# Row-tiled transposes, one copying engine, and one weight load on another queue, at the head of a SwiGLU kernel

## The chip, the cores and the metric

The kernel runs on one core of one Trainium2 chip. The time is device microseconds of one execution; the profile is one profiled execution of the same program.

## The reference

```python
# x: [1, 2048, 512], w_gate and w_up: [512, 1376], w_down: [1376, 512], all bf16
def reference(x, w_gate, w_up, w_down):
    g = _silu(x @ w_gate)
    u = x @ w_up
    return (g * u) @ w_down
```

## The kernel before

The 2048 tokens are worked in four chunks of 512. For each chunk the first stage computes the hidden tensor transposed: the 1376 hidden features are cut in ten F tiles of 128 and a rest of 96. For an F tile, TensorE multiplies four weight tiles of 128x128 (over the 512 input features) with the transposed input `xT_sb`, once for gate (a group "G") and once for up (a group "U"). Each group has one of the eight PSUM banks, in turn. ScalarE takes the silu of a gate bank, VectorE multiplies it with the up bank and stores bf16 in `hT_sb`. The rest of 96 features is packed in groups "X" and "Y". The second stage (lines 446 to 477) multiplies `hT_sb` with `w_down`, mostly in row tiles of 32, and stores the output.

Everything is scheduled by hand: each engine has one list of instructions in a fixed order, with waits on counting semaphores. The loads go out in the order written in `loads_on_scalar` and `loads_on_sync`, one hardware queue for each of the two engines. Gate and up weights are cut by F tiles in slabs, `slabs = [(0, 1), (1, 2), (2, 4), (4, 7), (7, NFT)]`: `load_gate(sp, 0, 1)` is the gate weights of F tile 0, and so on.

The head of the kernel concerns chunk 0. TensorE must have its input transposed. For most of x a transposing DMA does that (`load_x`). For the first 256 tokens this would land late, so they are loaded as they are (`load_xn`, two blocks of 128 tokens, `xn0` on SyncE's queue and `xn1` on ScalarE's) and transposed on TensorE against an identity matrix (line 357) into PSUM, and copied from there to `xT_sb`. A block `i` has two halves `h`: half 0 holds input features 0 to 255 (two weight tiles), half 1 the others. One copy moves one half; the copies of half 0 are on VectorE (line 300), those of half 1 on ScalarE (line 288), and `s_X` tells them how many transposes are done. While the loads are in flight TensorE runs matmuls on constants (`warm`, line 346): five of 512 columns and then `N_FILL` = 5 of 128 columns.

TensorE then runs groups 0 to 7 (gate and up of F tiles 0 to 3) for the first 256 tokens, in the order 0, 1, 2, 3, 4, 6, 5, 7: gate 0, up 0, gate 1, up 1, gate 2, gate 3, up 2, up 3. Gate 0 is done in two pieces of 128 tokens, each matmul waiting for the copy that it needs (`xt_ready`, line 336). After that the second 256 tokens of the same groups follow, gate 0 again in two pieces of 128 tokens, the first waiting for the load `x0b`, the second for `x0c`. From group 8 on the groups take all 512 tokens at once.

Of the kernel before, what the change touches and what calls it, by code (L numbers as in the profile page):

```python
# [7 lines left out]
FP32 = mybir.dt.float32  # L8

N_WARM = 5  # L10
N_FILL = 5


def bass_standalone__swiglu_ffn__prompt_kernel(nc, x, w_gate, w_up, w_down, out):
    _, S, D = x.shape
    F = w_gate.shape[1]
    P = 128
    KD = D // P
# [10 lines left out]
    NXN = HT // P  # L29
# [20 lines left out]
    with ExitStack() as es:  # L50
# [4 lines left out]
        xT_sb = sb("xT_sb", [P, KD, S], BF16)  # L55
# [14 lines left out]
        xn_sb = sb("xn_sb", [P, NXN, D], BF16)  # L70
# [3 lines left out]
        s_X = sem("s_X")  # L74
# [8 lines left out]
        def load_sem(name):  # L83
            loads[name] = sem(f"s_{name}")
            return loads[name]
# [6 lines left out]
        def load_x(eng, name, t0, t1):  # L92
            eng.dma_start_transpose(
                xT_sb[:, :, t0:t1], xf[t0:t1, :]
            ).then_inc(load_sem(name), 16)

        def load_w(eng, name, src, base, f0, f1):
            eng.dma_start(
                w_sb[:, :, base + f0:base + f1],
                src[:, f0:f1].rearrange("(k p) f -> p k f", p=P),  # L100
            ).then_inc(load_sem(name), 16)

        slabs = [(0, 1), (1, 2), (2, 4), (4, 7), (7, NFT)]
        slab_of = {ft: a for a, b in slabs for ft in range(a, b)}

        def load_gate(eng, a, b):
            load_w(eng, f"wg{a}", w_gate, 0, a * P, min(b * P, F))

        def load_up(eng, a, b):
            load_w(eng, f"wu{a}", w_up, UPH, a * P, min(b * P, F - 32))  # L110

        def load_xn(eng, i):
            eng.dma_start(xn_sb[:, i, :], xf[i * P:(i + 1) * P, :]).then_inc(load_sem(f"xn{i}"), 16)

        def loads_on_scalar(act):
            load_xn(act, 1)
            load_up(act, *slabs[0])

        def loads_on_sync(sp):
            load_xn(sp, 0)  # L120
            load_gate(sp, *slabs[0])
            for a, b in slabs[1:3]:
                load_gate(sp, a, b)
                load_up(sp, a, b)
            load_x(sp, "x0b", HT, HT + P)
            load_x(sp, "x0c", HT + P, SC)
            for a, b in slabs[3:]:
                load_gate(sp, a, b)
                load_up(sp, a, b)
            load_w(sp, "wut", w_up, F - (F - 32), F - 32, F)  # L130
            for c in range(1, NSC):
                load_x(sp, f"x{c}", c * SC, (c + 1) * SC)
            sp.dma_start(
                wd_sb[:, 0:NFF, :], w_down[0:NFF * P, :].rearrange("(k p) d -> p k d", p=P)
            ).then_inc(load_sem("wd"), 16)
            load_sem("wdt")
            for y0 in (0, 64):
                sp.dma_start(wd_sb[y0:y0 + 64, T01, :], w_down[NFF * P:F - SR, :]).then_inc(loads["wdt"], 16)
            for x0 in range(0, P, SR):
                sp.dma_start(wd_sb[x0:x0 + SR, T2, :], w_down[F - SR:F, :]).then_inc(loads["wdt"], 16)  # L140
            sp.dma_start(wd_sb[0:F_LAST, TAIL, :], w_down[NFF * P:F, :]).then_inc(load_sem("wdl"), 16)
# [12 lines left out]
        def add_op(eng, g, **what):  # L154
            n_read[eng] += 1
            op = dict(g=g, at=n_read[eng], **what)
            (act_ops if eng == "A" else dve_ops).append(op)
            g["readers"].append((eng, op["at"]))
            return op

        RT = [1] * NXN
        T_BANK = [2 * i for i in range(NXN)]

        def tview(i, h):
            n, b0 = RT[i], T_BANK[i] + RT[i] * h
            return bank_all[:, b0:b0 + n, 0:P // n].bitcast(BF16).rearrange("p b (k t) -> p k b t", k=2)

        sg_reader = []
# [42 lines left out]
                t_ready[c] = max(t_ready[c], d["at"])  # L211

        xt_ready = {}
        for i in range(NXN):
            for h, eng in enumerate("DA"):
                op = add_op(
                    eng, dict(readers=[]), kind="copy", ready=(s_X, 2 * sum(RT[:i]) + RT[i] * (h + 1)),
                    out=xT_sb[:, 2 * h:2 * h + 2, i * P:(i + 1) * P].rearrange("p k (b t) -> p k b t", b=RT[i]),
                    src=tview(i, h), stored=(None, 0),
                )  # L220
                xt_ready[i, h] = (eng, op["at"])

        for c in range(NSC):
            for ft in range(NFF):
# [8 lines left out]
        for at, t in enumerate(tiles):  # L233
# [3 lines left out]
            for c0, c1 in parts:  # L237
                g = add_group("O", t=t, c0=c0, c1=c1)
                eng = "A" if at % 2 == 1 and c0 == 0 else "D"
                op = add_op(  # L240
                    eng, g, kind="copy", out=o_sb[ob][:, c0:c1], src=g["bank"][:, 0:c1 - c0],
                    stored=(s_out[ob], need),
                )
# [15 lines left out]
        def on_sync(sp):  # L259
            loads_on_sync(sp)  # L260
            store_tiles(sp, "S")
            for i in range(NOS):
                sp.wait_ge(s_out[i], 16 * n_store[i])
# [11 lines left out]
        def on_scalar(act):  # L275
            loads_on_scalar(act)
            act.activation(adummy[:, 0:4], zero_c, ACT.Silu)
            for op in act_ops:
                act.wait_ge(*ready(op))
                if op["kind"] == "silu":  # L280
                    if op["free"]:
                        act.wait_ge(s_D, op["free"])
                    fn = ACT.Silu
                else:
                    if op["stored"][1]:
                        act.wait_ge(*op["stored"])
                    fn = ACT.Copy
                act.activation(op["out"], op["src"], fn).then_inc(s_A, 1)  # L288
            store_tiles(act, "A")
# [13 lines left out]
        def on_tensor(pe):  # L303
            landed = set()

            def need(name, count=1):
                if name not in landed:
                    pe.wait_ge(loads[name], 16 * count)
                    landed.add(name)
# [34 lines left out]
            def warm(n, width):  # L344
                for i in range(n):
                    pe.matmul(banks[NB - 1][:, 0:width], lhsT=ones_w, rhs=ones_m[:, 0:width], start=True, stop=True)  # L346

            warm(N_WARM, SC)
            warm(N_FILL, P)
            pe.wait_ge(s_I, 1)  # L350
            for i in range(NXN):
                need(f"xn{i}")
                for dk in range(KD):
                    for b in range(RT[i]):
                        rt = P // RT[i]
                        r0 = rt * b
                        ins = pe.matmul(  # L357
                            tview(i, dk // 2)[:, dk % 2, b, :], lhsT=xn_sb[r0:r0 + rt, i, dk * P:(dk + 1) * P],
                            rhs=ident[r0:r0 + rt, r0:r0 + rt], start=True, stop=True, is_transpose=True,
                            tile_position=(r0, 0), skip_group_check=True,  # L360
                        )
                        if dk % 2 == 1:
                            ins.then_inc(s_X, 1)

            first = groups[0:NB]
# [9 lines left out]
            for g in groups[NB:NO]:  # L375
                free(g)
                kind = g["kind"]
# [83 lines left out]
            for g in groups[NO + TPC * (TPC - 1):]:  # L461
                t, c0, c1 = g["t"], g["c0"], g["c1"]
# [5 lines left out]
                for fk in (tailed if last else full[1:]):  # L468
                    if fk < NFF:
                        h, w = hT_sb[:, fk, t * P:(t + 1) * P], wd_sb[:, fk, c0:c1]  # L470
                    else:
                        h, w = hl_sb[0:F_LAST, :], wd_sb[0:F_LAST, TAIL, c0:c1]
# [7 lines left out]
        on_gpsimd(nc.gpsimd)  # L480
        on_scalar(nc.scalar)
        on_tensor(nc.tensor)
        on_vector(nc.vector)

# [27 lines left out]
```

## Time and profile before

| | |
|---|---|
| median of 3 runs | 120.48 us |
| the runs | 120.21, 120.48, 120.73 us |
| the profiled execution | 119.86 us, span 118.6 us |
| PE busy | 115.4 us, 97% of the span |
| VectorE, ScalarE busy | 37.8 us, 34.9 us |
| transposes (line 357) | 8, started from 3.46 us on |
| first matmul of gate 0 (line 337) | 4.36 us |

In the views of the profile, PE is TensorE's matmuls and PEld its weight loads, DVE is VectorE, ACT ScalarE, POOL GpSimd; SPq and ACTq are the issuing sequencers of SyncE and ScalarE. Times are microseconds from the span's start. The name of a weight load in the trace, `w_sb<-in_w_gate_dram` or `w_sb<-in_w_up_dram`, does not say which slab it is; the order of issue does. q1 is the DMA queue of SyncE, q10 that of ScalarE. A matmul's time in the profile includes its way through the array, so neighbouring ones overlap: the distance of their starts is the pace.

### The profile page before, as it was taken

Reading aid. Unit: us, or ns where it says so; the run is one execution under the profiler, and the core shown is the slowest. Engines: PE = TensorE matmul, PEld = TensorE weight load, DVE = VectorE, ACT = ScalarE, POOL = GpSimd, SP = SyncE. Lnnn points to the kernel's source line nnn. Section 1 sums busy time; section 2 is a strip of 40 time slices with the busy share of each in tenths; the row PEclk is TensorE's granted clock in tenths of the full one; section 3 lists DMA queues with packets and bytes.
Section 4 is the critical chain, followed back from the end, with each engine's and each line's share of the span. In section 5 each row is a group of like instructions: output and inputs, shape, how many; then the busy total and the mean of one; then the engine's idle time right before and its main releaser. Section 6 shows DMA issues by size and latency. Waiting matters only on the chain.

```text
span 118.6 us, 2318 instructions
## 1 busy us (share of the span) xinstructions
PE 115.4 (97%) x1004; PEld 60.0 (51%) x1012; DVE 37.8 (32%) x58; ACT 34.9 (29%) x60; POOL 1.1 (1%) x7
## 2 busy tenths in 40 slices
PE   7999999999999999999999999999999999999993
PEld 2888444444444444444444444444444445885442
DVE  0106543344433444424444344360000044003321
ACT  4307324353244272343263432330000033003021
POOL 1000000000000000000000000010000000000000
DMA  3999999994000000000000000000000017200532
GB/s 104 270 200 330 267 172 188 233 358 105 0 6 0 0 0 0 0 0 6 0 0 6 0 0 0 0 0 6 0 6 0 0 57 239 68 0 0 168 103 88
DMA packets 17642, 8.83 MB, mean 74 GB/s; under 512 B 10624, under 2 KB 17632, under 8 KB 17632
## 3 DMA queue, kind: packets, MB, share of 16 engines
q1 hardware_dynamic: 16816, 8.33, 28.1%
q10 hardware_dynamic: 816, 0.36, 1.1%
q8 instruction: 8, 0.13, 0.4%
q14 instruction: 2, 0.02, 0.0%
HBM read 4.75 MB, written 2.10 MB: 58 GB/s over the span
## 4 chain that ended last, share of the span: by engine, by line
PE 97%; issue 1%; DVE 0%
PE bank L337 58%; PE bank L434 25%; PE bank L473 7%; PE bank L385 3%; PE bank L346 2%; PE bank L396 2%; PE bank L357 1%; DVE o_sb L300 0%
## 5 line engine op out<-in xcount | busy, mean ns | idle before, releaser
L337 PE MATMUL bank<-xT_sb,w_sb 128*128 128x512 bf16 (+2 forms) x355 | 69.9, 355 | 0.3
L337 PEld LDWEIGHTS bank<-xT_sb,w_sb 128*128 128x128 bf16 x360 | 34.4, 98 | 34.9
L296 DVE TENSOR_TENSOR hT_sb<-sg_sb,bank 128x512 bf16<-128x512 f32 x40 | 27.5, 688 | 40.5 <-PE bank L337 34.5
L288 ACT ACTIVATE sg_sb<-bank 128x512 f32<-128x512 f32 x40 | 23.8, 596 | 40.9 <-PE bank L337 40.9
L434 PE MATMUL bank<-wd_sb,hT_sb 32*128 32x512 bf16 x496 | 29.0, 374 | 0.0
L434 PEld LDWEIGHTS bank<-wd_sb,hT_sb 32*128 32x128 bf16 x496 | 15.3, 93 | 11.5 <-issue 0.4
L300 DVE CAST o_sb<-bank 128x512 bf16<-128x512 f32 (+1 forms) x10 | 5.7, 595 | 31.1 <-PE bank L434 25.9
L288 ACT ACTIVATE o_sb<-bank 128x512 bf16<-128x512 f32 (+1 forms) x8 | 4.3, 582 | 33.6 <-PE bank L434 27.9
L473 PE MATMUL bank<-wd_sb,hT_sb 128*128 128x512 bf16 (+2 forms) x55 | 7.9, 303 | 0.2 <-issue 0.2
L473 PEld LDWEIGHTS bank<-wd_sb,hT_sb 128*128 128x128 bf16 x56 | 4.2, 98 | 4.2 <-issue 0.4
L434 PE MATMUL bank<-wd_sb,hy_sb 32*128 32x512 bf16 (+1 forms) x32 | 5.0, 371 | 0.0
L385 PE MATMUL bank<-xT_sb,w_sb 128*128 128x512 bf16 x14 | 3.8, 379 | 0.1
L296 DVE TENSOR_TENSOR hx_sb<-sgx_sb,bank 32x512 bf16<-32x512 f32 x4 | 2.8, 691 | 3.5 <-ACT sgx_sb L288 3.5
L288 ACT ACTIVATE sgx_sb<-bank 32x512 f32<-32x512 f32 x4 | 2.4, 588 | 4.5 <-PE bank L385 4.5
L346 PE MATMUL bank<-const-bfloat16-1.0 128*128 128x512 bf16 (+1 forms) x10 | 2.8, 466 | 0.8 <-PEq L497 0.8
L434 PE MATMUL bank<-wd_sb,hx_sb 32*128 32x512 bf16 (+1 forms) x16 | 3.0, 371 | 0.0
L385 PEld LDWEIGHTS bank<-xT_sb,w_sb 128*128 128x128 bf16 x16 | 1.6, 98 | 1.9
L288 ACT ACTIVATE sgy_sb<-bank 64x512 f32<-64x512 f32 x4 | 2.4, 590 | 0.1
L346 PEld LDWEIGHTS bank<-const-bfloat16-1.0 128*128 128x128 bf16 x10 | 1.2, 139 | 2.2 <-issue 2.2
L396 PE MATMUL bank<-xT_sb,w_sb 128*64 128x512 bf16 x16 | 1.9, 382 | 0.0
L434 PEld LDWEIGHTS bank<-wd_sb,hy_sb 32*128 32x128 bf16 x32 | 1.6, 93 | 0.6
L300 DVE COPY xT_sb<-bank 128x256 bf16<-128x256 bf16 x2 | 0.6, 292 | 4.1 <-PE bank L357 3.9
(17 smaller groups left out, 8.9 us busy)
## 6 DMA issues: line engine op xcount, KB each, us to landing
out_dram<-o_sb SPq DMA_DIRECT2D x15, 128.0 KB, 1.8
wd_sb<-in_w_down_dram SPq DMA_DIRECT2D x1, 1280.0 KB, 8.1
w_sb<-in_w_gate_dram SPq DMA_DIRECT2D x1, 480.0 KB, 6.0
w_sb<-in_w_up_dram SPq DMA_DIRECT2D x1, 448.0 KB, 6.7
w_sb<-in_w_gate_dram SPq DMA_DIRECT2D x1, 384.0 KB, 3.9
w_sb<-in_w_up_dram SPq DMA_DIRECT2D x1, 384.0 KB, 4.3
w_sb<-in_w_gate_dram SPq DMA_DIRECT2D x2, 128.0 KB, 3.2
w_sb<-in_w_gate_dram SPq DMA_DIRECT2D x1, 256.0 KB, 3.5
```

The costliest lines, as they stand in the source:

```text
L288: act.activation(op["out"], op["src"], fn).then_inc(s_A, 1)
L296: ins = dve.tensor_tensor(op["out"], op["a"], op["b"], ALU.mult)
L300: ins = dve.tensor_copy(op["out"], op["src"])
L337: ins = pe.matmul(g["bank"][:, n0:n1], lhsT=w_sb[:, dk, col:col + P], rhs=xT_sb[:, dk, c * SC + n0:c * SC + n1], start=(dk == 0), stop=(dk ...
L346: pe.matmul(banks[NB - 1][:, 0:width], lhsT=ones_w, rhs=ones_m[:, 0:width], start=True, stop=True)
L357: ins = pe.matmul(tview(i, dk // 2)[:, dk % 2, b, :], lhsT=xn_sb[r0:r0 + rt, i, dk * P:(dk + 1) * P], rhs=ident[r0:r0 + rt, r0:r0 + rt], s ...
L385: ins = pe.matmul(g["bank"][:, :], lhsT=w_sb[:, dk, XC0:XC0 + P], rhs=xT_sb[:, dk, c * SC:(c + 1) * SC], start=(dk == 0), stop=(dk == KD - 1),
L396: ins = pe.matmul(g["bank"][y0:y1, :], lhsT=w_sb[:, dk, YC0:YC0 + 64], rhs=xT_sb[:, dk, c * SC:(c + 1) * SC], start=(dk == 0), stop=(dk == ...
L434: ins = pe.matmul(g["bank"][:, 0:c1 - c0], lhsT=h, rhs=wd_sb[r0:r0 + SR, w, c0:c1], start=(start and fk == fks[0]), stop=(stop and fk == f ...
L473: ins = pe.matmul(g["bank"][:, 0:c1 - c0], lhsT=h, rhs=w, start=(last and fk == 0), stop=(fk == (NFF if last else NFF - 1)), skip_group_ch ...
```

## The change

Three things. The fills are four instead of five. The load of up of F tile 1 is taken out of SyncE's list, where it stood behind gate 1, and becomes ScalarE's third load, behind `xn1` and up of F tile 0. And the transposes of three of the four halves are done in two row tiles of 64 tokens each: a half is then four transposes of 64 columns instead of two of 128, the two row tiles writing to two PSUM banks; the last half (block 1, half 1) keeps its two of 128. All four copies are on VectorE.

```diff
-N_FILL = 5
+N_FILL = 4
...
         def loads_on_scalar(act):
             load_xn(act, 1)
-            load_up(act, *slabs[0])
+            for a, b in slabs[:2]:
+                load_up(act, a, b)
 
         def loads_on_sync(sp):
             load_xn(sp, 0)
             load_gate(sp, *slabs[0])
-            for a, b in slabs[1:3]:
-                load_gate(sp, a, b)
-                load_up(sp, a, b)
+            load_gate(sp, *slabs[1])
+            load_gate(sp, *slabs[2])
+            load_up(sp, *slabs[2])
             load_x(sp, "x0b", HT, HT + P)
             load_x(sp, "x0c", HT + P, SC)
...
-        RT = [1] * NXN
-        T_BANK = [2 * i for i in range(NXN)]
+        halves = [(i, h) for i in range(NXN) for h in range(2)]
+        RT = {ih: 1 if ih == halves[-1] else 2 for ih in halves}
+        t_bank, t_count, nb, nt = {}, {}, 0, 0
+        for ih in halves:
+            t_bank[ih] = nb
+            nb += RT[ih]
+            nt += RT[ih]
+            t_count[ih] = nt
 
         def tview(i, h):
-            n, b0 = RT[i], T_BANK[i] + RT[i] * h
+            n, b0 = RT[i, h], t_bank[i, h]
...
         xt_ready = {}
-        for i in range(NXN):
-            for h, eng in enumerate("DA"):
-                op = add_op(
-                    eng, dict(readers=[]), kind="copy", ready=(s_X, 2 * sum(RT[:i]) + RT[i] * (h + 1)),
-                    out=xT_sb[:, 2 * h:2 * h + 2, i * P:(i + 1) * P].rearrange("p k (b t) -> p k b t", b=RT[i]),
-                    src=tview(i, h), stored=(None, 0),
-                )
-                xt_ready[i, h] = (eng, op["at"])
+        for i, h in halves:
+            op = add_op(
+                "D", dict(readers=[]), kind="copy", ready=(s_X, t_count[i, h]),
+                out=xT_sb[:, 2 * h:2 * h + 2, i * P:(i + 1) * P].rearrange("p k (b t) -> p k b t", b=RT[i, h]),
+                src=tview(i, h), stored=(None, 0),
+            )
+            xt_ready[i, h] = ("D", op["at"])
...
-            for i in range(NXN):
+            for i, h in halves:
                 need(f"xn{i}")
-                for dk in range(KD):
-                    for b in range(RT[i]):
-                        rt = P // RT[i]
+                rt = P // RT[i, h]
+                for k in range(2):
+                    dk = 2 * h + k
+                    for b in range(RT[i, h]):
                         r0 = rt * b
                         ins = pe.matmul(
-                            tview(i, dk // 2)[:, dk % 2, b, :], lhsT=xn_sb[r0:r0 + rt, i, dk * P:(dk + 1) * P],
+                            tview(i, h)[:, k, b, :], lhsT=xn_sb[r0:r0 + rt, i, dk * P:(dk + 1) * P],
                             rhs=ident[r0:r0 + rt, r0:r0 + rt], start=True, stop=True, is_transpose=True,
                             tile_position=(r0, 0), skip_group_check=True,
                         )
-                        if dk % 2 == 1:
+                        if k == 1:
                             ins.then_inc(s_X, 1)
```

## The prediction

> **What bounds the kernel now.** The page comes first: PE is busy for 115.4 of the 118.6 us, and the chain that ended last is PE for 97%. So a change pays only where PE waits. The chain of waits in order of time begins so (start us, us, what, count):
>
> ```profile
> 0.84 2.82 PE bank L346 x10
> 3.67 0.76 PE bank L357 x8
> 4.43 7.44 PE bank L337 x72
> 11.87 0.05 issue
> 11.92 10.31 PE bank L337 x47
> ```
>
> The change touches the first two pieces and the loads that feed the third. From 11.92 us PE needs 0.216 us for a matmul of 512 columns (10.36 us for the 48 of a neighbouring piece) and goes on so. Next the timeline of the head (start us, us, engine line):
>
> ```profile
> 2.27 0.51 SPq L98 DMA_DIRECT2D w_sb<-in_w_up_dram  x1
> ...
> 3.46 0.97 PE L357 MATMUL bank<-ident,xn_sb 128*128 128x128 bf16 x8
> 3.92 0.72 DVE L300 COPY xT_sb<-bank 128x256 bf16<-128x256 bf16 x2 [3.92 <-PE bank L357]
> ...
> 4.13 0.72 ACT L288 ACTIVATE xT_sb<-bank 128x256 bf16<-128x256 bf16 x2 [0.89 <-PE bank L357]
> ```
>
> Eight transposes start at 3.46; four copies follow on two engines, the last ending at 4.85 (4.13 + 0.72). The same timeline has gate 0's first matmul at 4.36 and up 0's first at 5.03. Gate 0's eight 128-column matmuls thus take 0.67 us. Undisturbed ones start 0.056 apart (four from 8.11 to 8.27 in a narrow window), 0.45 for eight, so gate 0 loses 0.22 us waiting for pieces of xT.
>
> Third, the loads, each in a window of its own, as issue time plus time to landing: xn 0 at 3.2, xn 1 at 3.4, gate 0 at 1.26 + 3.0 = 4.3, up 0 at 4.8, gate 1 at 1.73 + 3.4 = 5.1, up 1 at 2.27 + 3.3 = 5.6, slab 2 to 4 of gate at 2.83 + 3.5 = 6.3 and of up at 7.1, x0b at 3.92 + 3.9 = 7.8, x0c at 5.32 + 3.1 = 8.4. Gate 0's matmuls start 0.06 after gate 0 lands. From 5.03 to 8.11 PE runs 28 matmuls of 256 columns, 0.11 each, 0.44 for a group of four: gate 1 at 5.47, up 1 at 5.91, gate 2 at 6.35, gate 3, up 2, up 3, then gate 0's second half at 8.11. Set beside the landings: gate 2 begins 0.05 after its slab lands, and the last quarter of gate 0 (ideal start 8.33) begins at 8.42, 0.05 after x0c. PE is following the loads. The stretches, with DMA share and GB/s last, say why:
>
> ```profile
> 4.50:5.00 0.50, 0.50 (x8) 0.32 (x7) 0.14 (x1) 0.35 (x2) 0.00 (x0) 1.00 1.24 289
> ...
> 7.00:7.50 0.50, 0.50 (x7) 0.44 (x6) 0.00 (x0) 0.00 (x0) 0.00 (x0) 1.00 1.21 251
> 7.50:8.00 0.50, 0.50 (x8) 0.44 (x6) 0.00 (x0) 0.00 (x0) 0.00 (x0) 1.00 0.30 51
> ```
>
> From 2.5 to 7.5 us the 16 DMA engines are full (share 1.05 to 1.29 in every half microsecond), and they run dry only when x0c's packets are through. These loads are bound by bandwidth, not by issue. After 8.42 nothing stops PE again: slab 4 lands at 10.5 and is wanted at 11.7.
>
> **The change, part by part.** The profiled execution took 119.86 us: its span of 118.6 and 1.26 around it. The median of the runs shown is 120.48, 0.62 above; I work out shifts in the span and add them to the median.
>
> *One fill less.* Five fills run 2.93 to 3.67, starts 0.107 apart ((0.74 - 0.31) / 4). xn 0 is there at 3.2, so transposes may start at 3.36: 0.107 gained.
>
> *Transposes in row tiles.* Eight of 128 columns at 0.107 (0.86 us) become twelve of 64 columns and two of 128. By column count a short one is 0.053 (0.427 for 512, 0.107 for 128). Whether two of them run together no row shows for 64 rows. The nearest shows it for 32: 540 matmuls of line 434 in 29.41 us, 0.054 each where 512 columns alone take 0.216. So six pairs cost 0.32, plus 0.21 for the last two: 0.53, or 0.33 gained. Unpaired, 0.85: nothing. If a short one costs as much as a long one, 14 x 0.107 = 1.50: 0.64 lost. I take pairs.
>
> Against it stands the change of tile shape, twice (128 to 64 rows, and back for the last two). The timeline shows two such changes at full pace (last column of the first row: 16 matmuls):
>
> ```profile
> 77.42 1.92 PE L396 MATMUL bank<-xT_sb,w_sb 128*64 128x512 bf16 x16
> 79.27 0.40 PE L434 MATMUL bank<-wd_sb,hT_sb 32*128 32x512 bf16 x4
> ```
>
> Eight pairs at 0.216 are 1.73; from 77.42 to 79.27 are 1.85, so a change of shape costs about 0.10. PE here still runs at half pace (0.107 against 0.056), so 0.10 to 0.20 each; I take 0.10, by the row. The first eats the fill's 0.107: row tiles start at 3.46 as the transposes do now.
>
> *Copies, all on VectorE.* Each is 0.292 on VectorE (0.384 on ScalarE). Queued one behind another they overlap by 0.09 (two hy_sb multiplies of 0.683 fit in 1.29), so four take 0.92, or 1.17 without overlap. Reading two banks may be slower: the f32 casts give 0.224 for 64 columns and 0.688 for 512, 1.04 ns a column, so 0.42 for 256 without packing, and 1.4 to 1.7 for four. I take 0.292. The first half's last pair starts at 3.51, ends 0.26 later (0.311 less 0.053); the copy starts at 3.81; the last ends between 4.73 and 4.98, against 4.85 now. Two engines gave the same with eight slower transposes: the shorter transposes pay for the lost engine, and little is left. Gate 0 can't start before its weights, 4.3, anyway. Up 0 starts at 4.90 to 5.15; I take 4.95, 0.08 earlier. Behind the copies VectorE has nothing until the multiply at 9.56.
>
> *Up 1 on ScalarE.* The issue (0.5) goes ahead of the table load (1.74 to 3.02, then to about 3.5) and the dummy activation (to 3.7). ScalarE's next work is the silu at 8.85, now that its copies are gone: 5 us of cover, cost nothing. Every later SyncE issue comes 0.55 earlier. But the engines are full, and the bytes ahead of x0c are the same, so x0c lands where it did, give or take 0.1.
>
> What moves is the order. Up 1 used to follow gate 1 alone on SyncE's queue. Now it shares the engines, behind up 0, whose packets end about 4.3 (ScalarE's queue moves almost nothing from 4.25 on). While both queues worked, they shared nearly evenly:
>
> ```profile
> q1 hardware_dynamic: 518, 0.13, 59.3%
> q10 hardware_dynamic: 399, 0.11, 49.1%
> ```
>
> (2.75 to 3.75 us.) At 4.25 some 0.03 MB of gate 1 are left; they then take 0.25 us (0.06 MB at 250 GB/s) beside as much of up 1. The other 0.1 MB of up 1 go beside slab 2 to 4 of gate: 0.6 us at an even share, 0.9 at a third (its packets are 256 bytes beside 512). Packets end at 5.1 to 5.4, and a landing comes 0.65 after the last packet, as now (4.9 to 5.6): 5.8 to 6.1, 0.2 to 0.5 later than today. PE wants it at 4.95 + 0.88 = 5.83. I take 5.85 and a start at 5.90, against 5.91 now. Gate 2's slab, with the same bytes ahead of it, lands at 6.3 as before: PE at 6.35 as before, the last quarter at 8.42 as before.
>
> **Sum:** 0.08 gained at gate 0 is lost again at up 1 or gate 2; whatever is left is lost at x0c. Net 0.0, bounds -0.15 to +0.2: 120.5 us.
>
> **The rivals.** *Faster: x0c and the slabs land with their issue.* If the landing follows the issue, x0c comes up to 0.55 earlier and the 0.09 before the last quarter goes, with gate 0's 0.13 kept: 120.26. For it: x0c lands 1.8 us after its issue ends (5.32 + 1.26 = 6.58), as quickly as an output store. Against it: full engines until 7.5.
>
> *Slower: up 1 lands late.* The change says beside gate 1; it may land half a microsecond after it. At 6.1, up 1 starts at 6.15 and gate 2 at 6.59, 0.24 late, of which x0c's 0.09 hides a part: +0.15, 120.6. If slab 2 of up or x0c also slips by 0.2: 120.8. It decides once up 1 lands after 5.86. The Trainium skill (DMA: Bandwidth & Descriptors, Queues, rings and completion order) says that an engine alternates between queues by packets of several descriptors, not by bytes; by that up 1 gets the third and this rival holds. The window above (0.13 against 0.11 MB) had equal packet sizes on both queues for most of it and can't tell.
>
> *Slower: row tiles that don't overlap.* At 0.107 for each and slow copies, up 0 starts near 6.0: +0.97, less 0.09: 121.4. It decides once up 0 starts after 5.12. Against it: the rows of lines 434 and 396.
>
> *Slower: the clock.* Transpose starts are 0.107 apart, gate 0's 0.056: PE doubles its pace near 4.2, about 3.3 us after its first matmul, though the clock column reads 1.00 throughout. Now PE idles a little between the last transpose (4.1) and gate 0. If the half pace lasted another 3.3 us, half of that is lost: +1.65, 122.1. Against it: 0.2 us of idling in 3.3 is little. The Trainium skill (TensorE: Matmul & The Clock Gate, Part 4) says that a transpose does not count as PE activity in the way of a matmul; by that the stretch that counts shrinks from 2.62 us (0.84 to 3.46) to 2.51, which speaks for this rival. In the trace of before the pace doubled right after eight transposes, so those at least did not prevent it.
>
> **How the numbers follow.** No net change 0.64; faster by landings 0.14; up 1 late 0.10; row tiles alone 0.05; clock 0.07. The three runs spread 0.52 us. The likeliest is 120.5. The range, 119.95 (the faster case with half that spread) to 121.0 (late up 1 with it), leaves out the clock and about half of the row tiles and some 0.04 of tails. About 0.5%, 0.6 us, is what a measurement of this kernel can tell from no change: slower than that are the clock and most of the row tiles, 0.11; faster, past the 0.31 us that gate 0 (0.22) and x0c (0.09) lose now, only with the spread, 0.05; the rest, 0.84, within.
>
> **What would show it.** Right: row tiles from about 3.46 in pairs 0.05 apart, the last copy ending 4.7 to 5.0, up 0 at 4.9 to 5.1, up 1 landing at 5.8 or later, gate 2 near 6.35, the last quarter of gate 0 near 8.4. Wrong: x0c landing before 8.0, up 1 before 5.6, gate 2's slab before 6.1, or a pace of 0.107 beyond 4.4.

## The result, and the profile after

The changed kernel takes 120.85 us (median of 21 runs), the kernel before 120.48 us (also 21). The ratio is 1.003, with a 95% interval of 1.0016 to 1.0043: about 0.36 us slower. That is within the 0.5% that was forecast as most likely, on its slow side, and the interval tells it from no change at all. (One run of the changed kernel, 122.55 us, was a slow one and is not in the ratio.)

The profiled execution after has a span of 119.2 us against 118.6. Its chain of waits in order of time (start us, us, what, count) begins:

```profile
0.84 2.72 PE bank L352 x9
3.56 0.13 issue
3.69 0.83 PE bank L364 x14
4.53 18.34 PE bank L343 x120
```

Line 352 is the fills, 364 the transposes, 343 the gate and up groups (346, 357 and 337 before). There is no wait for a load in it. The transposes start at 3.69 us, not at 3.46, behind 0.13 us of waiting. From there on the chain shows no break in PE; it hides short ones, since neighbouring matmuls overlap, as the 0.18 us for which the first weight load of gate 0 waits. The timeline of the head:

```profile
1.25 1.08 ACTq L98 DMA_DIRECT2D w_sb<-in_w_up_dram  x2
1.26 1.52 SPq L98 DMA_DIRECT2D w_sb<-in_w_gate_dram  x3
2.36 1.28 ACT L283 ACT_TABLE_LOAD   x1 [2.36 <-issue]
...
3.69 0.83 PE L364 MATMUL bank<-ident,xn_sb 64*128 64x64 bf16 x14
4.03 0.89 DVE L306 COPY xT_sb<-bank 128x256 bf16<-128x256 bf16 x4 [4.03 <-PE bank L364]
4.44 4.62 PEld L343 LDWEIGHTS bank<-xT_sb,w_sb 128*128 128x128 bf16 x40 [0.18 <-DMA w_sb<-in_w_gate_dram]
```

Twelve short transposes start 0.026 apart (3.69 to 3.96), so two share a slot; four copies fit in 0.89 us. But gate 0 and what follows run at half pace: in the stretch from 5.3 to 6.2 us, and in the one from 6.7 to 8.7, the groups of PE are (count | busy us, mean ns):

```profile
L343 PE MATMUL bank<-xT_sb,w_sb 128*128 128x256 bf16 x5 | 1.2, 408 | 0.0
```

```profile
L343 PE MATMUL bank<-xT_sb,w_sb 128*128 128x256 bf16 x21 | 2.5, 273 | 0.0
```

The mean time of a matmul does not give the pace, the distance of the starts does: until about 6.2 us matmuls of 256 columns start 0.21 us apart, then 0.11. In the profile of before full pace was there from gate 0's first matmuls, at 4.36 us. Taken alone, these two profiles would say that the clock made the kernel slower. The experiments show that one kernel has the long half pace in one execution and not in the next, that the loss is there without it, and that it can be there without the loss.

Two executions are too few for this head. In thirteen profiles of kernels that differ only there, the span is always 106.9 us plus the start of group 8 (11.71 before, 12.35 after). All differences arise before that.

### The profile page after: what moved, and what is told of

Its sections match the earlier page's. It is cut to its first block, busy times and chain, and to the rows that moved or that the text cites. A ratio compares the mean times of both kernels' runs of the same rounds, so it can differ in the third digit from the quotient of the medians.

```text
span 119.2 us, 2336 instructions
## 1 busy us (share of the span) xinstructions
PE 116.5 (98%) x1017; PEld 60.2 (50%) x1017; DVE 38.2 (32%) x60; ACT 34.2 (29%) x58; POOL 1.1 (1%) x7
## 4 chain that ended last, share of the span: by engine, by line
PE 98%; DVE 0%; issue 0%
PE bank L343 59%; PE bank L441 25%; PE bank L480 7%; PE bank L392 3%; PE bank L352 2%; PE bank L403 2%; PE bank L364 1%; DVE o_sb L306 0%
## 5 line engine op out<-in xcount | busy, mean ns | idle before, releaser
L343 PE MATMUL bank<-xT_sb,w_sb 128*128 128x512 bf16 (+2 forms) x360 | 70.7, 359 | 0.0
L343 PEld LDWEIGHTS bank<-xT_sb,w_sb 128*128 128x128 bf16 x360 | 35.1, 99 | 34.8 <-DMA w_sb<-in_w_gate_dram 0.2
L392 PEld LDWEIGHTS bank<-xT_sb,w_sb 128*128 128x128 bf16 x16 | 1.6, 98 | 1.9
```

The source lines that it names most:

```text
L343: ins = pe.matmul(g["bank"][:, n0:n1], lhsT=w_sb[:, dk, col:col + P], rhs=xT_sb[:, dk, c * SC + n0:c * SC + n1], start=(dk == 0), stop=(dk ...
L392: ins = pe.matmul(g["bank"][:, :], lhsT=w_sb[:, dk, XC0:XC0 + P], rhs=xT_sb[:, dk, c * SC:(c + 1) * SC], start=(dk == 0), stop=(dk == KD - 1),
```

## The experiments

The theories after the two profiles: *clock* (idle time before gate 0 brings the half pace back), *loads* (up 1 and what is behind it land later), *chance* (the two executions differ by accident).

**The changed kernel again.**

> The changed kernel once more, for a second profile. Clock theory: PE's pace falls back to half (0.107 us for 128 columns, 0.21 for 256) somewhere between 4.4 and 6.5 us again, and the span is 119.2 to 119.9 us, 120.85 us in the timing. Load theory (the late x0c and up 1 set the time): the pace is full from about 4.2 us on, and PE waits at up 1 and at the last quarter of gate 0. Chance theory (the profiled execution had slow loads at 2.0 to 2.5 us by accident): xn 0 lands at 3.2 and the head looks like that of before.

120.75 us, ratio to before 1.0025 (1.0011 to 1.004). PE is at full pace at 4.5 us here, and still the span is 119.5 us. The clock theory's half pace did not come back; xn 0 landed at 3.57, so this was not a head like the first one of before either. Its chain of waits:

```profile
1.71 0.03 issue
1.74 5.10 DMA w_sb<-in_w_up_dram
6.84 0.05 issue
6.88 5.86 PE bank L343 x56
```

The chain goes back through ScalarE's third load: up 1 is issued at 1.74 and lands at 6.84. The same profile's timeline shows both stops, at gate 1 and at up 1:

```profile
6.03 0.61 PE L343 MATMUL bank<-xT_sb,w_sb 128*128 128x256 bf16 x4 [0.33 <-DMA w_sb<-in_w_gate_dram]
...
6.88 2.36 PE L343 MATMUL bank<-xT_sb,w_sb 128*128 128x256 bf16 x20 [0.24 <-DMA w_sb<-in_w_up_dram]
```

**Transposes of 128 tokens.**

```diff
-        RT = {ih: 1 if ih == halves[-1] else 2 for ih in halves}
+        RT = {ih: 1 for ih in halves}
```

> The changed kernel with all transposes of 128 tokens (eight, as before); one fill less, copies on VectorE and up 1 on ScalarE stay. Clock theory: the transposes take 0.86 us instead of 0.5 and fill the gap before gate 0, so the half pace does not come back; 0.2 to 0.5 us faster than the changed kernel, about 120.5. Load theory: no difference from the changed kernel, 120.8.

120.67 us, ratio 1.0018 (1.0003 to 1.0033), not to be told from the changed kernel. PE was at full pace from about 4.5 us, and stood waiting for gate 1 (6.23) and up 1 (6.93). The eight transposes cost 0.107 each again, and it made no difference.

**Up 1 back on SyncE's queue.**

```diff
-            for a, b in slabs[:2]:
-                load_up(act, a, b)
+            load_up(act, *slabs[0])
...
-            load_gate(sp, *slabs[1])
-            load_gate(sp, *slabs[2])
-            load_up(sp, *slabs[2])
+            for a, b in slabs[1:3]:
+                load_gate(sp, a, b)
+                load_up(sp, a, b)
```

> The changed kernel with up of F tile 1 back in SyncE's list behind gate 1. Load theory: up 1 lands 0.3 to 0.5 us earlier (5.6 to 5.8) and the kernel gains 0.2 to 0.4 us, to 120.5. Clock theory: the half pace after 4.4 us stays, 120.8 within 0.15 us.

120.41 us, ratio 1.000 (0.9983 to 1.0018): the loss is gone. Up 1 landed at 5.66, 0.62 after gate 1. The half pace lasted until 6.2 us in this profile, as in the first one after. In this execution it cost about 0.5 us: slab 2 to 4 of gate landed at 6.50, and PE came to it at 7.08. The median of the 12 runs is none the slower for it.

**Five fills.**

> The changed kernel with five fills of 128 columns instead of four. Clock theory: the gap before the transposes closes by 0.107 us and part of the gain of a busy PE comes back: 0.1 to 0.4 us faster than the changed kernel, 120.5. Load theory: no difference, 120.8; the fill ends at 3.46, before xn 0 can be used where it lands late.

120.65 us, ratio 1.0023 (1.0006 to 1.004): the same as with four. In this profile the row tiles started at 3.69 again, behind xn 0 at 3.56; the number of fills does not set their start.

**The kernel before again, and the move alone.**

> The kernel before, for a second profile. If the first profile's early input (xn 0 at 3.22 us) was an accident, xn 0 lands near 3.57 us here as in the four others, and the span is near 119.2 us, gate 1 at 5.0 to 5.2 and up 1 at 5.5 to 5.7 as before. If early input belongs to that kernel, 3.2 again and a span of 118.6.

Span 119.3 us, xn 0 at 3.68. The first profile of before was an early execution. Here gate 1 landed at 5.91 and not at 5.1 (a miss of both expectations), up 1 at 6.36, and the chain of waits goes through slab 2 to 4 of gate ("slab 2" from here on):

```profile
2.27 0.51 SPq L98
2.78 0.04 issue
2.82 4.30 DMA w_sb<-in_w_gate_dram
7.13 0.05 issue
7.17 5.42 PE bank L337 x52
```

The kernel before with up 1 on ScalarE, and nothing else changed:

> The kernel before with only the move of up 1 to ScalarE's queue; fills, transposes and copies as before. Load theory: the whole loss comes back, ratio 1.002 to 1.004, about 120.75 us, gate 1 landing at 5.4 to 6.2 and up 1 at 6.1 to 6.9. If the loss needs the other parts too (the row tiles or the single copying engine): ratio 1.000 within 0.0015.

120.77 us, ratio 1.0032 (1.0008 to 1.0056): the whole loss, without row tiles and with two copying engines. Gate 1 landed early in this execution, at 5.17, and up 1 at 6.42 all the same. The timeline has the transposes at full pace already (eight starts 0.055 apart), and the stop:

```profile
3.75 0.61 PE L358 MATMUL bank<-ident,xn_sb 128*128 128x128 bf16 x8
4.49 1.54 PE L338 MATMUL bank<-xT_sb,w_sb 128*128 128x128 bf16 x16
6.47 1.70 PE L338 MATMUL bank<-xT_sb,w_sb 128*128 128x256 bf16 x14 [0.43 <-DMA w_sb<-in_w_up_dram]
```

**Slab 2 to 4 held back.**

```diff
         def load_sem(name):
-            loads[name] = sem(f"s_{name}")
+            if name not in loads:
+                loads[name] = sem(f"s_{name}")
             return loads[name]
...
             load_gate(sp, *slabs[1])
+            sp.wait_ge(load_sem("wu1"), 16)
             load_gate(sp, *slabs[2])
```

> The changed kernel, but SyncE issues slab 2 to 4 of gate, and all behind it, only when up 1 has landed. Only gate 1 is then beside up 1. Sharing theory (up 1 and gate 1 are late because slab 2's packets go between theirs): gate 1 lands at 5.0 to 5.3 and up 1 at 5.4 to 5.8; the kernel as a whole gets slower by about 1.5 us, since slab 2 then lands near 8.5. Queue theory (ScalarE's queue is slow with a third load, whatever stands beside it): up 1 at 6.1 to 6.9 still.

Gate 1 at 5.36, a little later than expected, up 1 at 5.54, 0.18 later, in one execution. So ScalarE's queue is not slow by itself; what comes between is slab 2 of SyncE's queue. The two queues from 4.5 to 5.5 us (packets, MB, share of the engines), first in the second profile of the changed kernel, then with slab 2 held:

```profile
q10 hardware_dynamic: 349, 0.09, 43.7%
q1 hardware_dynamic: 253, 0.11, 40.3%
```

```profile
q10 hardware_dynamic: 406, 0.10, 48.0%
q1 hardware_dynamic: 76, 0.02, 8.0%
```

Without slab 2, SyncE's queue is nearly done. Up 1's queue moves about as much in this microsecond with slab 2 beside it as without; the difference comes behind it. With slab 2 held, up 1's packets are through by 5.25 us. In the second profile of the changed kernel 109 are left at 5.5, and from 5.5 to 6.9 us they go beside 939 of SyncE's queue:

```profile
q1 hardware_dynamic: 939, 0.43, 115.3%
q10 hardware_dynamic: 109, 0.03, 8.3%
```

The last of them ends at 6.48: the last fifth of the load takes a whole microsecond. The kernel with slab 2 held took 122.37 us as a whole, as slab 2 then came at 8.39.

**PE kept busy.** Up 1 on SyncE's queue, and more matmuls on constants before and behind the transposes:

```diff
-N_FILL = 4
+N_FILL = 7
+N_KEEP = 1
...
+            warm(N_KEEP, P)
```

> The changed kernel with up 1 back on SyncE's queue, seven fills instead of four, and one matmul of 128 columns more on constants between the transposes and gate 0, so that PE has no gap from 0.84 us on. Gap theory (idle time before gate 0 is what keeps PE at half pace until 6 us or later): the half pace ends by 4.5 us, and 0.2 to 0.4 us faster than the kernel before, 120.1. Phase theory (the end of the half pace falls where it falls, between 4.2 and 7 us, in each execution anew): 120.4, ratio 1.000 within 0.002.

120.52 us, ratio 0.9997 (0.9976 to 1.0018). The half pace ended at about 5.2 us. Some 0.14 us of idling were left before the transposes, as xn 0 landed at 3.59. A busier PE bought nothing.

**Two more profiles of each kernel.** After the profiles so far it seemed that the whole stream of loads, not up 1 alone, came 0.3 us later with up 1 on ScalarE.

> A third profile of the kernel before. Order theory (only up 1 is put back, the rest of the stream keeps its time): over all profiles slab 2 of gate and x0c land on average as late with up 1 on SyncE's queue as on ScalarE's, 6.75 and 8.7 us here. Stream theory (two queues side by side deliver everything behind them later): they land 0.3 us earlier here on average; up 1 0.4 to 0.6 us after gate 1 in both theories.

> A fourth profile of the kernel before, for the same averages: slab 2 of gate near 6.75 us, x0c near 8.7 us, up 1 0.4 to 0.6 us after gate 1.

> A third profile of the changed kernel. Both theories: up 1 lands 0.7 us or more after gate 1. Stream theory: slab 2 of gate near 7.05 us, x0c near 9.05 us on average. Order theory: 6.75 and 8.7.

> A fourth profile of the changed kernel, for the same averages: up 1 0.7 us or more after gate 1; stream theory: slab 2 of gate near 7.05 us, x0c near 9.05 us; order theory: 6.75 and 8.7.

These four executions took 120.66 and 120.84 us before, 120.39 and 120.31 after: single runs of both kernels spread over more than the difference (before 119.88 to 120.94, after 120.11 to 121.16). The landings of all profiles but the one with slab 2 held (us, issue plus time to landing):

| up 1 on | kernel | gate 1 | up 1 | between | slab 2 of gate | x0c |
|---|---|---|---|---|---|---|
| SyncE | before | 5.11 | 5.56 | 0.45 | 6.30 | 8.37 |
| | before again | 5.91 | 6.36 | 0.45 | 7.13 | 9.01 |
| | before, third profile | 5.95 | 6.43 | 0.48 | 7.19 | 9.07 |
| | before, fourth profile | 6.21 | 6.65 | 0.44 | 7.38 | 9.31 |
| | changed, up 1 back | 5.04 | 5.66 | 0.62 | 6.50 | 8.43 |
| | PE kept busy | 5.89 | 6.33 | 0.44 | 7.08 | 9.00 |
| | *mean* | 5.69 | 6.17 | 0.48 | 6.93 | 8.87 |
| ScalarE | changed | 5.42 | 6.15 | 0.73 | 6.73 | 8.77 |
| | changed again | 5.99 | 6.84 | 0.85 | 7.20 | 9.23 |
| | changed, third profile | 5.61 | 6.16 | 0.55 | 6.80 | 8.86 |
| | changed, fourth profile | 5.74 | 6.42 | 0.68 | 6.77 | 8.81 |
| | transposes of 128 | 6.23 | 6.93 | 0.70 | 7.33 | 9.33 |
| | five fills | 6.05 | 6.87 | 0.82 | 7.27 | 9.24 |
| | before, up 1 moved | 5.17 | 6.42 | 1.25 | 6.79 | 8.80 |
| | *mean* | 5.74 | 6.54 | 0.80 | 6.98 | 9.01 |

Up 1 comes 0.32 us later behind gate 1 on average (0.80 less 0.48). Slab 2 of gate is 0.05 later, x0c 0.14, in columns that spread over a microsecond: the stream theory's 0.3 us is not borne out. Within one execution the columns are steadier. Counted from slab 2, x0c comes 1.97 to 2.06 us later in all seven profiles with up 1 moved, and 1.88 to 1.93 in five of the six with up 1 on SyncE's queue (2.07 in the first of before). So x0c does lose about 0.1 us; why, no run here shows. The third and fourth profile after missed the 0.7 that was expected between gate 1 and up 1 (0.55 and 0.68).

## Why the prediction was right or wrong

The forecast held by its width: 120.85 us is in the range, and 0.3% is within the half per cent. Its sum of 0.0 with bounds of -0.15 to +0.2 was too low; 0.36 us went the way of the rival in which up 1 lands late, past that rival's first price of 120.6 and near its second of 120.8. (The lower end of the range, 120.26 less half of 0.52, is 120.0 and not 119.95.)

That is in part luck. Of the signs named for being right, the first profile after showed the pairs, the last copy (4.91) and up 1 at 5.8 or later (6.15). But the row tiles started at 3.69, not 3.46, up 0 at 5.27, not 4.9 to 5.1, gate 2 at 7.10, not 6.35, and the last quarter of gate 0 at 9.07, not 8.4; and a pace of 0.107 beyond 4.4 us, named as a sign of being wrong, was there.

*The baseline.* Every landing of before was read from one execution that turned out early: its gate 1 at 5.1 us is 5.9 to 6.2 in the other three of the same kernel, xn 0 at 3.2 is 3.58 to 3.69. The profiled time, 0.62 us below the median, hinted at it, and it was used for the sum only, not to question the landings.

*One fill less* was worth nothing, where 0.107 was counted. The step that failed is that xn 0 is there when the fills end. It landed at 3.56 us or later in all profiles but the first of before and the one with slab 2 held (3.40), and the changed kernel's fills end before that (the last starts at 3.25).

*Row tiles in pairs* was right, 0.026 us for each. The change of shape before the last two cost 0.14 (3.99, where the next pair would start, to 4.13), within the 0.10 to 0.20 given; the first change hid behind the wait for xn 0. The rival of row tiles that don't overlap falls.

*Four copies on one engine* was right: 0.281 to 0.292 each, the last ending at 4.91, where 4.73 to 4.98 was given. (Four of 0.292 with three overlaps of 0.09 are 0.90, not the 0.92 of the prediction; 0.89 was measured.) Two banks cost nothing more. From the landing of xn 0 to the end of the last copy the changed kernel needs about 1.35 us in all four of its profiles, the kernel before 1.56 to 1.63. The new head is 0.2 us shorter, and that does not show in the time. All this head work, with up 1 left on SyncE, comes to a ratio of 1.000: gate 0 waits for gate 0's weights or the input, and the groups behind it for theirs.

*Up 1.* The difference was right and its consequence mis-sized. Given were 0.2 to 0.5 us later than on SyncE's queue; measured are 0.37 between the means. But the sum took 5.85 from that range and let up 1 start at 5.90, "against 5.91 now", so that nothing was lost; it landed at 6.15 to 6.93. Counted from gate 1, 5.85 is 0.74 later, close to the 0.80 measured; it is PE's place that was wrong. In the early execution PE came to up 1 0.80 us after gate 1 had landed (5.91 and 5.11), so the delay was hidden. In most of the others gate 1 lands so late that PE stands there waiting, and then PE wants up 1 0.44 us after gate 1. On SyncE's queue up 1 keeps that rhythm (0.48), on ScalarE's it does not (0.80). That slab 2's packets come between is shown by the kernel that holds them back. Two terms of the landing were wrong in opposite directions: up 1's packets were to end at 5.1 to 5.4 and ended at 5.8 to 6.6, and the landing was to follow 0.65 us later and followed after 0.32 to 0.37. The Trainium skill (DMA: Bandwidth & Descriptors, Queues, rings and completion order) has the queues served in turn by packets; the trace agrees in so far as both queues worked side by side from 4.5 to 5.5 us with 44% and 40% of the engines' time. In that microsecond up 1 did not get only a third of the bytes: 0.09 MB against 0.11. Part of SyncE's packets there were still gate 1's, of the same size, and the tail behind 5.5 us got far less, so no run here tests the third.

*Faster, by landings that follow the issue,* falls: SyncE's issues came 0.55 earlier, and x0c landed at 8.77 at the earliest. The loads are bound by bandwidth in the main, as said; but in the second profile after the engines were busy for only 0.71 of the stretch from 4.5 to 5.0 us, where the first of before has 1.24.

*The clock.* The half pace does last until 6.2 us or longer in some executions, as the rival had it, with up 1 on SyncE's queue as well. With more matmuls on constants around the transposes it ended at 5.2 us. It ended before 3.75 us in one execution and at 6.8 in another, of kernels that run the same matmuls until 3.25 us. It can hold PE back: in the first profile after, the last quarter of gate 0 began at 9.07, where x0c, landed at 8.77, would have let it begin at 8.82. But it is not what the timed runs show, since the kernel with up 1 back on SyncE's queue has it in its profile, and a ratio of 1.000. Whether row tiles have a part in it stays open: it lasted past 5.6 us in four of the eight profiles with row tiles and in none of the six with transposes of 128 tokens. The Trainium skill (TensorE: Matmul & The Clock Gate, Part 4) says that the full clock does not engage for transposes, as they do not count as PE activity in the same way. The kernel before with up 1 moved does not agree with the first half, with eight transposes 0.055 apart; the second half is not tested by it, as the pace had doubled before the first of them.

*What stays open.* The timed runs put the whole loss on the move of up 1 (1.0032 for it alone, 1.000 for the rest). How it becomes 0.36 us, the profiles do not show. Up 1 lands 0.37 us later in them, and in three of seven the chain of waits goes through it. But where it does, x0c would have stopped PE almost as long. In the second profile after, PE goes on from up 1 without a stop and begins the last quarter of gate 0 at 9.30; x0c landed at 9.23, and PE starts 0.05 us after a landing. So up 1 alone costs 0.02 us there, and 0.01 to 0.04 in the other two. The 0.1 us that x0c loses behind slab 2 comes on top. The profiles do not have the loss itself either: their spans have a mean of 119.24 us over the six with up 1 on SyncE's queue and 119.29 over the seven with it moved. Of the moved kernels, executions of 120.31 to 120.83 us were profiled, and the timed ones reach 121.28. What makes those slower is not shown.

## What to carry to other kernels

When the DMA engines are nearly full, taking a load off a queue need not speed it up: it changes who goes first. Within SyncE's queue the loads arrived in the order in which they were wanted. The load moved to a second queue shared with what was meant to come after it, and it was the early one that paid. Read landings from several executions before working with tenths of a microsecond, and distrust them where the profiled time is off the median.

## What the runs showed of the hardware

The first load of an execution landed at 3.22 to 3.69 us, after an issue that was always at 0.81. A load issued at 1.73 us (gate 1) landed at 5.04 to 6.23. The pace of PE doubled at 3.75 us or earlier in one execution and at 6.8 us in another, in kernels whose PE began at 0.84 us, while the clock in the profile read 1.00 throughout. Transposes of 64x64 in two row tiles started 0.026 us apart at half pace. A landing came 0.32 to 0.37 us after the last packet of a load of 128 KB (up 1 on ScalarE's queue).
